# Pairwise additions of a state-space kernel's factors move to GpSimd, and its contractions take half the matmuls

## The chip, the cores and the metric

The program runs on one core of one Trainium2 chip. The metric is the device time of one execution in microseconds. TensorE (PE in the profile) multiplies, with weight loads shown as PEld; VectorE is DVE, ScalarE is ACT, GpSimd is POOL, SyncE (SP) issues most of the transfers.

## The reference

Four residual blocks on one sequence of 2048 positions and 640 channels: attention, state space (S4D), attention, state space. Both attention blocks use the same weights, and both state-space blocks the same parameters.

```python
x = x + A(layernorm(x), wqkv, wo)   # 32 heads of 20: softmax(q k^T * Dh**-0.5) v, then @ wo
x = x + B(layernorm(x), ...)        # below
x = x + A(layernorm(x), wqkv, wo)
x = x + B(layernorm(x), ...)

# B: one convolution kernel K per channel d, from 128 complex states n
A = -exp(log_A_real) + 1j * A_imag
C = (C_real + 1j * C_imag) * dt
P = exp(A * dt * arange(L))
K = 2 * einsum("dn,dnl->dl", C, P).real       # 640 x 2048
y = irfft(rfft(u, 2L) * rfft(K, 2L))[:L] + u * D_skip
```

## The kernel before

**The stages.** First comes a stretch of layer norms, transposes and the first q, k and v products; then attention one; its output product with the norm of the state-space block, and the transform of K beside it; the state-space block; and the same again without K, which is kept in DRAM (`kha`, `khb`).

**Attention.** There are 8 groups of 4 heads with 4 query blocks each, so 32 blocks; a block has 16 key tiles of 2 halves. One half is a *wave*: `scores` makes eight matmuls into a PSUM tile `S` and one exponential `pt<-S` of 128x1024 on ScalarE (L778). One attention therefore has 1024 waves. `values` (L792) multiplies the exponentials with V into `pa`. At the end of a block VectorE empties `pa` (`oc<-pa`, `oc<-oc,pa`), the row sums go through DRAM on GpSimd's DMA queue (`dn<-oc`, `dr<-dn`, then a reciprocal on VectorE, `dn<-dr`, `db<-dn`), and at the end of the next block VectorE scales (`oc<-oc,db`) and GpSimd stores (`ot<-oc`). The remaining q, k and v products run between waves as *jobs* (`m<-xh,wh` and others, L560 and L524), emptied by VectorE (`qc`, `sq`, `qhi`, `qlo`, `V`).

**The convolution kernel, `kgen`.** It runs inside attention one as a *filler*. It makes K for 32 channels at a time (20 times, index `k`), eight channels in each of 4 `sub` portions: 80 portions in all. `expand` builds a table of powers `ktab` with some thirty small VectorE operations per `k`. `left` makes, once for two portions, the complex left factors `ka` (real and imaginary part) in six VectorE operations of 128x512: four products and two operations that combine them. `right` makes four products `kb` of 128x512 by four VectorE operations, and these are not combined: `contract` lets TensorE add them up in PSUM, with four matmuls for each channel. VectorE copies the result to `ko`, and after four portions GpSimd stores it (`kd<-ko`).

```python
for c8 in range(DC // 4):
    if c8:
        yield plan.pe + 0.7, 0.43, True, ()
    plan.on_pe(0.43)
    for n in range(4):                       # ts[0..3] of right, ka re/re/im/im
        for j in range(4):
            chain(te.matmul(ps[...], a[n // 2][:, ch, :], b[n][:, dd, :], start=(n == 0), stop=(n == 3), ...))
```

**What sets the order.** A planner (`Plan`) keeps the assumed time of TensorE, ScalarE and VectorE in `pe`, `act` and `dve`, and the program is written in that order; the order is then held by dependencies without waits (`tie`, `chain`). Each VectorE operation is put down with 0.07 us plus its elements per partition over 960. `weave` takes the next step of the filler while `plan.dve < plan.pe + 0.2`. A finished portion is queued in `pend` with the time at which it is ready, and `slot` puts its contraction between two waves when that time has come and the jobs are far enough ahead (`ahead`); at most one portion waits while the next is made. `Ordered` wraps VectorE, GpSimd and SyncE: every VectorE operation is counted and ordered, on GpSimd and SyncE only transfers, memsets and `partition_all_reduce` are ordered. For each of the five blocks of q and k, `longest` calls that reduction on GpSimd (`k2m<-k`), `shift` uses its result on VectorE.

When the filler and the jobs are done, `end_jobs` frees their memory and loads the output weights (`wot`); GpSimd splits them (`woh<-wot`, `wol<-wot,woh`, L938 and L939).

Of the kernel before, what the change touches and what calls it, by code (L numbers as in the profile page):

```python
# [11 lines left out]
F32 = mybir.dt.float32  # L12
# [4 lines left out]
ALU = mybir.AluOpType  # L17
# [29 lines left out]
class Plan:  # L47


    def __init__(self):  # L50
        self.pe = self.act = self.dve = 0.0
        self.keep = False

    def on_pe(self, cost, after=0.0):
# [4 lines left out]
class Ordered:  # L59
# [4 lines left out]

    def __getattr__(self, name):
        f = getattr(self.engine, name)
        if name not in ("dma_start", "memset", "partition_all_reduce") and not self.count:
            return f

        def call(out, *a, **k):  # L70
            if self.count:
                big = a[0].shape if "reduce" in name else out.shape
                self.plan.dve = max(self.plan.dve, self.plan.pe - 0.9) + 0.07 + math.prod(big[1:]) / 960
            made = f(out, *a, **k)  # L74
            if self.plan.keep:
                self.last = self.tie(made, self.last)
            return made
        return call
# [3 lines left out]
def mha_s4d_kernel(ctx, tc, x_in, wqkv, wo, lar, aim, cr, ci, ldt, dsk,  # L82
                   c_e1, c_eb, c_f2, c_fa, c_sel, c_lv, c_id, c_sg, c_e16, c_f16, c_id16, out, parts="asas", general=None):
    nc = tc.nc
    plan = Plan()

    def tie(made, before):

        if before is not None:
            tc.add_manual_dep(made.ins, before.name, mybir.DependencyInfo(  # L90
                mybir.DependencyClass.NoSync, mybir.DependencyReason.DATA), reason="order")
        return made.ins

    se, te = nc.scalar, nc.tensor
    ve, ge, sy = (Ordered(e, plan, tie, e is nc.vector) for e in (nc.vector, nc.gpsimd, nc.sync))
# [10 lines left out]
    def pst(pool, *a, **k):  # L106
        return ps_[pool].tile(*a, **k)
# [68 lines left out]
    def chain(ins):  # L176
        last[0] = tie(ins, last[0])

    def kgen():
        NL = len(LV)  # L180
        BC, DC = 32, 8
# [59 lines left out]
        def load_powers(k):  # L241
            ge.dma_start(kpw[k % 2].rearrange("p r n d -> p (r n) d"),
                         wd[:, :, :, k * BC:k * BC + BC].rearrange("p r n d -> p (r n) d"))
# [21 lines left out]
        def views(tab, dd, hi, lo, shp):  # L265
            return ([tab[:, r, dd, hi].unsqueeze(3).to_broadcast(shp) for r in range(2)],
                    [tab[:, r, dd, lo].unsqueeze(2).to_broadcast(shp) for r in range(2)])

        def left(tab, half, out):

            shp = [P, AC, 4, 8]
            fa, fb = views(tab, slice(half * AC, half * AC + AC), slice(24, 28), slice(16, 24), shp)
            re, im = (p2.tile(shp, F32, name=f"ka{j}") for j in range(2))
            t = p3.tile(shp, F32, name="kat")
            out.extend(a.rearrange("p d h l -> p d (h l)") for a in (re, im))
            ve.tensor_mul(re, fa[0], fb[0])
            yield
            ve.tensor_mul(t, fa[1], fb[1])
            yield
            ve.tensor_sub(re, re, t)  # L280
            yield
            ve.tensor_mul(im, fa[0], fb[1])
            yield
            ve.tensor_mul(t, fa[1], fb[0])
            yield
            ve.scalar_tensor_tensor(im, im, -1.0, t, ALU.mult, ALU.subtract)
            yield

        def right(tab, neg, sub, out):

            shp = [P, DC, 8, 8]
            fa, fb = views(tab, slice(sub * DC, sub * DC + DC), slice(8, 16), slice(0, 8), shp)
            ts = [p2.tile(shp, F32, name=f"kb{j}") for j in range(4)]
            out.extend(a.rearrange("p d h l -> p d (h l)") for a in ts)
            ve.tensor_mul(ts[0], fa[0], fb[0])
            yield
            ve.tensor_mul(ts[1], neg[:, sub * DC:sub * DC + DC].unsqueeze(3).to_broadcast(shp), fb[1])
            yield
            ve.tensor_mul(ts[2], fa[0], fb[1])
            yield  # L300
            ve.tensor_mul(ts[3], fa[1], fb[0])
            yield

        def contract(r, bs, sub, ko, a, b):

            ps = pst("M", [P, 512], F32, tag=f"m{r}", name=f"m{r}")[:, :DC // 4 * NB].rearrange("p (c b) -> p c b", b=NB)
            for c8 in range(DC // 4):
                if c8:
                    yield plan.pe + 0.7, 0.43, True, ()
                plan.on_pe(0.43)  # L310
                for n in range(4):
                    for j in range(4):
                        ch, dd = DC * (sub % 2) + 4 * c8 + j, 4 * c8 + j
                        chain(te.matmul(ps[32 * j:32 * j + 32, c8, :], a[n // 2][:, ch, :], b[n][:, dd, :],  # L314
                                        start=(n == 0), stop=(n == 3), tile_position=(0, 32 * j)))
            evac = lambda: ve.tensor_copy(ko[:, 2 * sub:2 * sub + 2, :], ps)
            emptied(*((None, evac) if r else (evac,)))
            if sub == BC // DC - 1:
                ge.dma_start(kd[bs, :].rearrange("(c j) (a b) -> (j a) c b", j=4, b=NB), ko)

        NE, NSUB, AC = D // BC, BC // DC, 2 * DC
        for n in range(0, NL, 2):
# [11 lines left out]
        p3 = kw3.__enter__()  # L334
        kw2 = tc.tile_pool(name="kw2", bufs=2, side="right")
        p2 = kw2.__enter__()
        neg = p3.tile([P, BC, 8], F32, name="kneg")
# [6 lines left out]
        for k in range(NE):  # L344
            ko = p2.tile([P, BC // 4, NB], F32, name="ko")
            bs = slice(k * BC, k * BC + BC)
            for sub in range(NSUB):
                if sub % 2 == 0:
                    a = []
                    yield from left(tab, sub // 2, a)  # L350
                b = []
                yield from right(tab, neg, sub, b)
                pend.append((plan.dve, contract, (bs, sub, ko, a, b)))
                while len(pend) > 1:
                    yield "wait"
            if k + 1 < NE:
                yield from expand(k + 1, kpw[(k + 1) % 2], tab, neg)
                if k + 3 < NE:
                    load_powers(k + 3)
# [7 lines left out]
    pend = []  # L367
    free = [0.0, 0.0]
    part = [None, None]
    busy = lambda: part[0] is not None  # L370

    def emptied(*copies):

        for r, f in enumerate(copies):
            if f:
                plan.dve = max(plan.dve, plan.pe + 0.25)
                f()
                free[r] = plan.dve + 0.15
# [12 lines left out]
    def attention(x, stats):  # L391
# [218 lines left out]
        def ahead(wave):  # L610

            for (w0, c0), (w1, c1) in zip(AHEAD, AHEAD[1:]):
                if wave <= w1:
                    return c0 + (c1 - c0) * (wave - w0) / (w1 - w0)
            return c1
# [7 lines left out]
        def slot(until=None):  # L623

            if head[0] is None:
                head[0] = next(todo[0], None)
            begun = head[0] and head[0][2]
            if pend and part[0] is None and not begun and (head[0] is None or spent[0] >= ahead(len(ends) - 2)):
                t, f, args = pend[0]
                r = free.index(min(free))  # L630
                t = max(t + 0.15, free[r])
                if t <= plan.pe or until is None and head[0] is None:
                    part[:] = f(r, *args), (t, 0.43, True, ())
                    pend.pop(0)
            step = part[1] if part[0] else head[0]
            if step is None:
                return False
            t = max([step[0], *(free[r] for r in step[3])])
            if until and (t > plan.pe or plan.pe + step[1] > until):
                return False  # L640
            plan.on_pe(0.0, t)
            if part[0]:
                part[1] = next(part[0], None)
                if part[1] is None:
                    part[0] = None
            else:
                spent[0] += step[1]
                head[0] = next(todo[0], None)
            return True
# [6 lines left out]
        def need(*what):  # L656

            while not have.issuperset(what):
                if not slot():
                    assert fins  # L660
                for b in what:
                    if head[0] is None or not head[0][2]:
                        finish(b)

        with ExitStack() as c2:
# [37 lines left out]
            if first_layer:  # L703
                filler[:2] = kgen(), False
                weave(1)
            sy.dma_start(self_, c_sel)
            for i4 in range(4):
# [10 lines left out]
                for i in range(4):  # L718
                    t = xr[i] if x is None else xp.tile([P, D], F32, tag=f"xr{i}", name=f"xn{i}")
# [700 lines left out]
```

## Time and profile before

| | |
|---|---|
| three runs | 2769.9, 2770.72, 2777.75 us (median 2770.72) |
| profiled execution, span | 2775.8 us, 117573 instructions; its own time is not listed apart from its span, which lies 5.1 us above the median |
| busy: PE, ACT, DVE, POOL | 92%, 85%, 53%, 30% of the span |
| mean granted TensorE clock | 0.987 |
| attention one, first to last wave | 112 to 1146 us |
| filler: first to last contraction | 145 to 1030 us |
| output product, transform of K, state space one | 1146 to 1483 us |
| attention two, first to last wave | 1564 to 2545 us |

The shares over the whole span average stages with different limits; the stretch that matters here is from about 235 to 1030 us, in which the filler runs beside attention. A DVE, POOL or PE line of the groups with L74 stands for the helper that records every ordered operation, so groups are told apart by their tiles. A matmul of f32 operands counts as two records.

### The profile page before, as it was taken

The numbers are of one execution on the slowest core, as the hardware profiler recorded it, in microseconds if no ns is written. First come the engines' busy times: TensorE is split into PE (matmuls) and PEld (weight loads), VectorE is DVE, ScalarE is ACT, GpSimd is POOL, SyncE is SP. The second block draws the span as 40 slices with busy tenths as digits, with TensorE's granted clock in tenths as the row PEclk, the third lists the DMA queues.
The fourth block names the chain that finished last, engine by engine and source line by source line (L and its number), as shares of the span: only waits on it lengthen the run. The fifth ranks groups of instructions, "written<-read, shape, count | busy, mean of one in ns | idle before, by whom it ended". The sixth has DMA issues, their size and how long they took to land.

```text
span 2775.8 us, 117573 instructions
## 1 busy us (share of the span) xinstructions
PE 2544.2 (92%) x51968; PEld 1436.6 (52%) x51968; DVE 1469.0 (53%) x3292; ACT 2352.1 (85%) x2781; POOL 821.2 (30%) x1232
## 2 busy tenths in 40 slices
PE   7898989999999997899999998999999888878998
PEld 3453544444444442587796544544444333335988
DVE  8645778978887870366777333332222100002865
ACT  8797989999999998645665698999999999997464
POOL 1112222323223324300573022222322422222376
PEclk9999999999999999999999999999999999999999
DMA  6512232323222223354543112111211211112365
GB/s 230 162 43 68 54 77 52 85 59 78 56 68 55 57 84 96 100 202 179 198 150 92 34 49 66 54 52 51 55 50 38 69 27 38 39 40 71 106 194 159
DMA packets 179128, 238.65 MB, mean 86 GB/s; under 512 B 36144, under 2 KB 124208, under 8 KB 176816
## 3 DMA queue, kind: packets, MB, share of 16 engines
q1 hardware_dynamic: 143168, 184.44, 20.6%
q0 software_dynamic: 35440, 46.58, 7.8%
q8 instruction: 410, 6.72, 1.0%
q14 instruction: 110, 0.90, 0.1%
HBM read 154.87 MB, written 76.03 MB: 83 GB/s over the span
## 4 chain that ended last, share of the span: by engine, by line
ACT 46%; PE 28%; issue 11%; DVE 7%; DMA 6%; POOL 1%; SPq 0%; ACTq 0%; DVEq 0%; POOLq 0%
ACT pt L778 46%; PE pa L792 4%; PE S L775 3%; PE psv L1148 3%; PE po L1054 3%; PE psy L1158 2%; PE psx L1136 2%; PE psx L1113 2%; PE po L1048 1%; DMA kop<-ks 1%; PE m L314 1%; PE pv L524 1%; PE pst L1123 1%; PE m L560 1%; PE pq L681 1%
## 5 line engine op out<-in xcount | busy, mean ns | idle before, releaser
L778 ACT ACTIVATE pt<-S 128x1024 f32<-128x1024 f32 x2048 | 1930.9, 1041 | 71.8 <-PE S L775 57.2
L792 PE MATMUL pa<-pt,V 64*32 64x512 f32 x16384 | 1099.6, 594 | 0.6 <-DVE oc L74 0.6
L775 PE MATMUL S<-qop,kop 61*32 61x512 f16 x16384 | 869.4, 383 | 160.6 <-ACT pt L778 138.0
L775 PEld LDWEIGHTS <-kop 61*32 61x32 f16 x16384 | 369.9, 90 | 830.7 <-issue 726.1
L74 POOL DMA_DIRECT2D dn<-oc x256 | 125.2, 496 | 835.6 <-DVE oc L74 768.2
L792 PEld LDWEIGHTS pa<-pt,V 64*32 64x32 f32 x16384 | 308.9, 107 | 69.4 <-issue 8.3
L74 DVE COPY oc<-pa 128x512 f32<-128x512 f32 x64 | 44.2, 691 | 414.8 <-PE pa L792 414.7
L74 DVE TENSOR_SCALAR qc<-m 128x512 f32<-128x512 f32 x64 | 44.1, 689 | 289.2 <-PE m L560 289.2
L74 POOL DMA_DIRECT2D db<-dn x256 | 129.3, 511 | 139.7 <-DMA dn<-dr 137.0
L74 DVE TENSOR_TENSOR kb<-ktab 128x512 f32<-128x512 f32 x240 | 155.3, 684 | 1.5 <-PE m L314 1.5
L560 PE MATMUL m<-xh,wh 64*32 64x512 f16 x2560 | 139.1, 380 | 3.0 <-DVE qc L74 3.0
L560 PE MATMUL m<-xh,wl 64*32 64x512 f16 x2560 | 138.3, 378 | 0.7 <-issue 0.7
L560 PE MATMUL m<-xl,wh 64*32 64x512 f16 x2560 | 138.4, 378 | 0.0
L74 POOL DMA_DIRECT2D ot<-oc x256 | 130.7, 517 | 8.9 <-DVE oc L74 6.0
L314 PEld LDWEIGHTS m<-kb,ka 128*32 128x32 f32 x5120 | 79.8, 110 | 101.6 <-issue 64.5
L560 PEld LDWEIGHTS <-wh 64*32 64x32 f16 x5120 | 87.7, 94 | 75.4 <-issue 37.6
L1141 POOL TENSOR_TENSOR t<-t,kb 128x512 f32<-128x512 f32 x80 | 102.1, 1276 | 70.3 <-DVE t L74 69.4
L1125 ACT COPY xt<-pst 128x1024 f16<-128x1024 f16 x80 | 81.6, 1023 | 46.7 <-PE pst L1123 46.5
L314 PE MATMUL m<-kb,ka 128*32 128x64 f32 x5120 | 105.8, 224 | 11.4 <-DVE qc L74 11.4
L74 POOL DMA_DIRECT2D dn<-dr x64 | 35.7, 557 | 234.1 <-DVE dr L74 229.8
L1142 POOL TENSOR_TENSOR t<-t,t 128x512 f32<-128x512 f32 x78 | 99.3, 1273 | 7.3 <-DVE t L74 1.3
L970 POOL TENSOR_TENSOR ul<-u,uh 128x640 f16<-128x640 f32 x30 | 46.5, 1566 | 177.7 <-ACT uh L969 177.7
(273 smaller groups left out, 3770.4 us busy)
## 6 DMA issues: line engine op xcount, KB each, us to landing
ka<-kha SPq DMA_DIRECT2D x80, 256.0 KB
kb<-khb SPq DMA_DIRECT2D x80, 256.0 KB
db<-dn POOLq DMA_DIRECT2D x256, 64.0 KB, 2.8
kpw<-wd POOLq DMA_DIRECT2D x20, 576.0 KB, 7.7
qop<-qs SPq DMA_DIRECT2D x256, 40.0 KB
kop<-ks SPq DMA_DIRECT2D x128, 80.0 KB
ot<-oc POOLq DMA_DIRECT2D x256, 40.0 KB, 2.6
otl<-ot SPq DMA_DIRECT2D x32, 320.0 KB
```

The source lines that it names most:

```text
L74: made = f(out, *a, **k)
L314: chain(te.matmul(ps[32 * j:32 * j + 32, c8, :], a[n // 2][:, ch, :], b[n][:, dd, :], start=(n == 0), stop=(n == 3), tile_position=(0, 32 ...
L560: chain(te.matmul(ps[r][32 * t:32 * t + 32, :], a_[rows, ct, 32 * t:32 * t + 32], m[rows, ct, sl], start=(k == 0), stop=(k == 14), tile_po ...
L775: chain(te.matmul(S[32 * t:32 * t + 32, 512 * r:512 * r + 512], kt_[rows, kc + 32 * t:kc + 32 * t + 32], qt[rows, :], start=True, stop=Tru ...
L778: se.activation(pt, S, AF.Exp, scale=SCALE)
L792: chain(te.matmul(pa[r][32 * j:32 * j + 32, :], V[rows, kt, VP * h:VP * h + 32], pts[j // 2][rows, 512 * (j % 2):512 * (j % 2) + 512], sta ...
L1054: te.matmul(pos[hf], oh[:, ct, :], m[:, ct, 320 * hf:320 * hf + 320], start=False, stop=(ct == NCT - 1 and m is wol))
L1113: te.matmul(ps[:, r, i, :], e1[:, e, s, r, :], m[:, s, bs], start=(n == 0), stop=(n == 2))
L1125: se.copy(xt, pt.rearrange("p k g c -> p k (g c)"))
L1141: ge.tensor_mul(t2, t2, kb)
L1142: (ge if g0 else ve).tensor_add(t1, t1, t2)
L1148: te.matmul(pv[:, g].rearrange("p r i c -> p (r i c)"), t1[:, g * P:g * P + P], fa, start=True, stop=True)
```

## The change

`left` and `right` no longer leave all additions to VectorE and TensorE: GpSimd adds or subtracts the products in pairs. Two of the six VectorE operations of `left` go to GpSimd. `right` keeps its four VectorE products and gets two GpSimd operations, after which two combined tiles remain, and `contract` has two matmuls for each channel instead of four, put down as one portion of 0.5 us where there were two of 0.43 us. The tiles `ts[1]`, `ts[3]` and the second operands of `left` have one buffer each. The planner has a time for GpSimd (`pool`), and a portion is ready by that time. GpSimd's `tensor_add` and `tensor_sub` are ordered too, wherever they occur while the order is kept. Every VectorE operation is put down with 0.15 us instead of 0.07 us, in both attentions.

```diff
-                self.plan.dve = max(self.plan.dve, self.plan.pe - 0.9) + 0.07 + math.prod(big[1:]) / 960
+                self.plan.dve = max(self.plan.dve, self.plan.pe - 0.9) + 0.15 + math.prod(big[1:]) / 960
+            elif pool:
+                self.plan.pool = max(self.plan.pool, self.plan.dve + 0.15) + 1.3
...
         def left(tab, half, out):
-            t = p3.tile(shp, F32, name="kat")
+            t, t_ = (p3.tile(shp, F32, name=f"kat{j}") for j in range(2))
             ve.tensor_mul(re, fa[0], fb[0])
             yield
             ve.tensor_mul(t, fa[1], fb[1])
-            yield
-            ve.tensor_sub(re, re, t)
+            ge.tensor_sub(re, re, t)
             yield
             ve.tensor_mul(im, fa[0], fb[1])
             yield
-            ve.tensor_mul(t, fa[1], fb[0])
-            yield
-            ve.scalar_tensor_tensor(im, im, -1.0, t, ALU.mult, ALU.subtract)
+            ve.tensor_mul(t_, fa[1], fb[0])
+            ge.tensor_add(im, im, t_)
...
         def right(tab, neg, sub, out):
-            ts = [p2.tile(shp, F32, name=f"kb{j}") for j in range(4)]
-            out.extend(a.rearrange("p d h l -> p d (h l)") for a in ts)
+            fn = neg[:, sub * DC:sub * DC + DC].unsqueeze(3).to_broadcast(shp)
+            ts = [(p3 if j % 2 else p2).tile(shp, F32, name=f"kb{j}") for j in range(4)]
+            out.extend(a.rearrange("p d h l -> p d (h l)") for a in ts[::2])
             ve.tensor_mul(ts[0], fa[0], fb[0])
             yield
-            ve.tensor_mul(ts[1], neg[...], fb[1])
+            ve.tensor_mul(ts[1], fn, fb[1])
+            ge.tensor_add(ts[0], ts[0], ts[1])
             yield
             ve.tensor_mul(ts[2], fa[0], fb[1])
             yield
-            ve.tensor_mul(ts[3], fa[1], fb[0])
+            ve.tensor_mul(ts[3], fn, fb[0])
+            ge.tensor_sub(ts[2], ts[3], ts[2])
...
         def contract(r, bs, sub, ko, a, b):
+            plan.on_pe(0.5)
             for c8 in range(DC // 4):
-                if c8:
-                    yield plan.pe + 0.7, 0.43, True, ()
-                plan.on_pe(0.43)
-                for n in range(4):
+                for n in range(2):
...
-                pend.append((plan.dve, contract, (bs, sub, ko, a, b)))
+                pend.append((plan.pool, contract, (bs, sub, ko, a, b)))
...
-                    part[:] = f(r, *args), (t, 0.43, True, ())
+                    part[:] = f(r, *args), (t, 0.5, True, ())
```

More of the change, by code (lines that the diff above doesn't have):

```diff
@@ L50, in __init__ @@
     def __init__(self):
-        self.pe = self.act = self.dve = 0.0
+        self.pe = self.act = self.dve = self.pool = 0.0
         self.keep = False
@@ L66, in __getattr__ @@
         f = getattr(self.engine, name)
-        if name not in ("dma_start", "memset", "partition_all_reduce") and not self.count:
+        pool = name in ("tensor_add", "tensor_sub")
+        if name not in ("dma_start", "memset", "partition_all_reduce") and not self.count and not pool:
             return f
@@ L292, in right @@
             fa, fb = views(tab, slice(sub * DC, sub * DC + DC), slice(8, 16), slice(0, 8), shp)
-            ts = [p2.tile(shp, F32, name=f"kb{j}") for j in range(4)]
-            out.extend(a.rearrange("p d h l -> p d (h l)") for a in ts)
+            fn = neg[:, sub * DC:sub * DC + DC].unsqueeze(3).to_broadcast(shp)
+            ts = [(p3 if j % 2 else p2).tile(shp, F32, name=f"kb{j}") for j in range(4)]
+            out.extend(a.rearrange("p d h l -> p d (h l)") for a in ts[::2])
             ve.tensor_mul(ts[0], fa[0], fb[0])
             yield
-            ve.tensor_mul(ts[1], neg[:, sub * DC:sub * DC + DC].unsqueeze(3).to_broadcast(shp), fb[1])
+            ve.tensor_mul(ts[1], fn, fb[1])
+            ge.tensor_add(ts[0], ts[0], ts[1])
             yield
@@ L306, in contract @@
             ps = pst("M", [P, 512], F32, tag=f"m{r}", name=f"m{r}")[:, :DC // 4 * NB].rearrange("p (c b) -> p c b", b=NB)
+            plan.on_pe(0.5)
             for c8 in range(DC // 4):
-                if c8:
-                    yield plan.pe + 0.7, 0.43, True, ()
-                plan.on_pe(0.43)
-                for n in range(4):
+                for n in range(2):
                     for j in range(4):
                         ch, dd = DC * (sub % 2) + 4 * c8 + j, 4 * c8 + j
-                        chain(te.matmul(ps[32 * j:32 * j + 32, c8, :], a[n // 2][:, ch, :], b[n][:, dd, :],
-                                        start=(n == 0), stop=(n == 3), tile_position=(0, 32 * j)))
+                        chain(te.matmul(ps[32 * j:32 * j + 32, c8, :], a[n][:, ch, :], b[n][:, dd, :],
+                                        start=(n == 0), stop=(n == 1), tile_position=(0, 32 * j)))
             evac = lambda: ve.tensor_copy(ko[:, 2 * sub:2 * sub + 2, :], ps)
@@ L319, in contract @@
                 ge.dma_start(kd[bs, :].rearrange("(c j) (a b) -> (j a) c b", j=4, b=NB), ko)
+            yield from ()
         NE, NSUB, AC = D // BC, BC // DC, 2 * DC
```

## The prediction

> **What bounds the kernel now.** I read the page first, for the chain that ended last, then the windows of attention one and two, then the waits of the stretch with the filler, and last the groups by form for prices.
>
> ```profile
> span 2775.8 us, 117573 instructions
> ACT 46%; PE 28%; issue 11%; DVE 7%; DMA 6%; POOL 1%; SPq 0%; ACTq 0%; DVEq 0%; POOLq 0%
> ...
> 235.00:1030.00 795.00, 753.25 (x20788) 358.93 (x20781) 653.56 (x1427) 755.64 (x791) 235.81 (x401) 0.99 0.27 64
> 1030.00:1146.00 116.00, 88.45 (x1860) 35.99 (x1852) 8.96 (x19) 106.73 (x117) 35.91 (x58) 0.96 0.27 88
> 1685.00:2180.00 495.00, 473.97 (x11440) 229.77 (x11439) 146.57 (x278) 480.63 (x510) 121.08 (x239) 0.99 0.18 52
> ...
> 2180.00:2479.00 299.00, 172.62 (x2600) 49.29 (x2592) 298.91 (x325) 1.00 0.15 40
> ```
>
> The second block of rows is from the windows: stretch, its length, then busy time and count of PE, PEld, DVE, ACT, POOL, then clock, DMA share, GB/s. The last row is a window of the exponentials and what touches them alone. ScalarE's exponentials lead the chain with 46%. Undisturbed they take 299 / 325 = 0.920 us each. With jobs but no filler (1685 to 2180) it is 495 / 510 = 0.97; with jobs and filler (235 to 1030) 795 / 791 = 1.005. So the filler's stretch holds 795 - 791 x 0.92 = 67 us over the bare exponentials, and in it no engine has much room: PE 95% busy, ACT 95%, DVE 82%. This is all that can be won or lost there: an engine that grows past ScalarE's pace becomes the bound.
>
> ```profile
> ACT pt L778 <- PE S L775: 29.4, 21, 5.9
> ...
> DVE oc L74 <- PE pa L792: 38.2, 20, 6.9
> DVE ko L74 <- PE m L314: 30.3, 52, 1.8
> DVE qc L74 <- PE m L560: 29.0, 8, 6.9
> DVE dr L74 <- DMA dr<-dn: 14.2, 6, 4.6
> ```
>
> These are the waits of the same stretch (total, times, longest). VectorE's idle 141 us (795 - 654) are mostly waits in its fixed order for TensorE's results, 97.5 us in three rows. They can't simply be filled: an operation behind such a wait comes after it.
>
> **The change, part by part.** *Removed from VectorE.* Two of six operations of `left`, forty times each:
>
> ```profile
> L74 DVE TENSOR_TENSOR ka<-ka,kat 128x512 f32<-128x512 f32 x40 | 27.6, 690 | 1.2
> L74 DVE SCALAR_TENSOR_TENSOR ka<-ka,kat 128x512 f32<-128x512 f32 x40 | 27.4, 685 | 1.0
> L74 DVE TENSOR_TENSOR kb<-ktab 128x512 f32<-128x512 f32 x240 | 155.3, 684 | 1.5 <-PE m L314 1.5
> L314 PE MATMUL m<-kb,ka 128*32 128x64 f32 x5120 | 105.8, 224 | 11.4 <-DVE qc L74 11.4
> L1141 POOL TENSOR_TENSOR t<-t,kb 128x512 f32<-128x512 f32 x80 | 102.1, 1276 | 70.3 <-DVE t L74 69.4
> L74 DVE TENSOR_TENSOR oc<-oc,db 128x512 f32<-128x512 f32 x64 | 44.5, 695 | 24.7 <-DMA dn<-oc 22.0 <-DMA db<-dn 2.7
> ```
>
> That is 27.6 + 27.4 = 55 us, of which some 54 lie in the stretch. *Removed from TensorE:* 2560 of 5120 records, 53 us of 105.8 us busy. TensorE is late only where it, and not VectorE, sets the pace. At best the filler's stretch falls to about 0.955 per wave, between the 0.97 and the 0.92 above.
>
> *Where the work goes.* The built order of the changed kernel puts the last contraction behind 992 waves, where it stands behind 909 of 1024 now. The filler's stretch, from wave 120 (235 us), becomes 872 waves long: 872 x 0.92 = 802 us bare, 833 us at 0.955, 876 us at the present 1.005. VectorE's own work in it is 653.6 - 54 + 5 = 605 us, the 5 for two and a half more blocks of three operations of 0.7 us (`oc`).
>
> *Added to GpSimd:* 80 additions for `left` and 160 for `right`, 240 x 1.276 = 306 us, some 298 in the stretch. GpSimd was 236 of 795 us busy, so it has the time. What matters is what they do to VectorE while they run:
>
> ```profile
> 1349.32 1.28 POOL L1141 TENSOR_TENSOR t<-t,kb 128x512 f32<-128x512 f32 x1 [11.91 <-DVE t L74]
> 1350.64 0.69 DVE L74 TENSOR_TENSOR t<-t,t 128x512 f32<-128x512 f32 x1 [0.28 <-POOL t L1141]
> 1352.07 1.27 POOL L1141 TENSOR_TENSOR t<-t,kb 128x512 f32<-128x512 f32 x1 [1.46 <-DVE t L74]
> 1352.47 0.68 DVE L74 TENSOR_TENSOR x<-psx,x 128x512 f16<-128x512 f32 x1
> 2633.52 2.50 POOL L1141 TENSOR_TENSOR t<-t,kb 128x512 f32<-128x512 f32 x2 [12.02 <-DVE t L74]
> 2634.84 1.74 DVE L74 TENSOR_TENSOR t<-t,t 128x512 f32<-128x512 f32 x1 [0.22 <-POOL t L1141]
> ...
> L970 POOL TENSOR_TENSOR ul<-u,uh x30: 1394/1416/2087, 1166.2 to 2620.1; 128x640 f16<-128x640 f32 x30
> L74 DVE TENSOR_TENSOR ol<-otl,oh x32: 807/825/1674, 1126.5 to 2611.0; 128x640 fp32r<-128x640 f32 x32
> ```
>
> The first six rows are from the timeline (start, duration), the last two give the shortest, median and longest in ns. At 1350.64 VectorE's addition of two tiles in SBUF runs just after GpSimd's, and takes 0.69 us. At 2634.84 the same addition starts while GpSimd's second multiplication runs, and takes 1.74: it ends 0.56 us after GpSimd does, so it has waited. An operation with one input in PSUM (`x<-psx,x`, 1352.47) runs in the middle of a GpSimd operation and takes its usual 0.68. The last two rows show it from both sides, `ul` up to 2087 instead of 1416, `ol` up to 1674 instead of 825. So a GpSimd addition and a VectorE operation with two SBUF inputs take turns, and the price to VectorE is 1.74 - 0.69 = 1.05 us where it meets one from the start.
>
> [...]
>
> Nearly all of `kgen` is of this kind. Of the 240 additions, in VectorE's built order, 200 have such an operation directly behind the product that releases them (it has started, so GpSimd waits), and 157 have one again as the second behind (it meets the running addition). With 97.5% of them in the stretch: none blocked 605 us of VectorE work; all 234 blocked 605 + 246 = 851; the 157 in full and the other 83 for half, 605 + 161 + 42 = 808. I take 808, because the order and not the mean decides who meets whom. VectorE is 82% busy now; with later results it waits less, so I take 91%: 808 / 0.91 = 888 us, against 876 at the present pace. The ends are 833 (VectorE not the bound) and 851 / 0.91 = 935.
>
> *A cost that the diff does not show.* GpSimd loads another library where it goes from the cross-partition reduction to additions:
>
> ```profile
> 1032.16 0.72 POOL L938 CAST woh<-wot 128x640 fp32r<-128x640 f32 x1 [5.58 <-DMA wot<-in_wo]
> 1043.21 1.55 POOL L939 TENSOR_TENSOR wol<-wot,woh 128x640 fp32r<-128x640 f32 x1 [10.33 <-issue]
> 2194.41 1.53 POOL L939 TENSOR_TENSOR wol<-wot,woh 128x640 fp32r<-128x640 f32 x1 [8.95 <-issue]
> ```
>
> The built order has a library instruction ahead of `wol`, whose inputs had been ready for 10.33 us and 8.95 us. Now there is one such return in each attention. In the changed order the reductions of blocks 1 to 4 stand among the additions, so there are four more: 4 x 9.6 = 38 us of GpSimd. Queued behind each are additions, `dn`, `ot` and `kd` transfers. VectorE waits for it as soon as it writes a one-buffer tile (`ts[1]`) whose addition is outstanding, and TensorE at the contraction. After block 2 the next such product stands some ten operations behind the reduction, so nearly all is felt; after 1, 3 and 4 a whole `expand` of small operations lies between and hides half or more. I take 20 us, between 0 and 38.
>
> [...]
>
> *The sums' way through DRAM* (`dn`, `dr`, `db`, four steps on GpSimd for each block) now stands between additions that wait for products. The planner has no term for these issues. VectorE waited 14.2 us for `dr` in 6 cases; I take 6 us more, between 0 and 28 blocks x 1.3 us = 36.
>
> *The last 32 waves and the rest.* After the filler come 32 x 0.92 = 29 us. The output weights are loaded and split only there, with 11 us of GpSimd work but no library load, and the end of attention one now holds them. I take 8 us, between 0 and 16. Attention two has no filler; the higher count reorders its jobs a little: 0, within 8 either way.
>
> *Sum,* from wave 120 to the end of attention one: now 1146 - 235 = 911 us; then 888 + 20 + 6 + 29 + 8 = 951. That is +40 us: the profiled execution would go from a span of 2775.8 to 2816. The median of the runs lies 5.1 below that span, so I give 2770.7 + 40 = 2811 us.
>
> **The rivals.** *Faster.* VectorE's waits for TensorE (97.5 us) and its operations on PSUM cover the additions, and TensorE, freed of 53 us, sets a better pace. For it: the 29.4 us in which ScalarE waits for S and TensorE's 95%. Against it: the order (147 additions have two such operations in a row behind their product). It decides once fewer than about 40% of the additions block (605 + 98 = 703 us, the VectorE share of now). Time: 833 + 0 to 8 for reloads + 29 + 8 = 878, so -33; with a third of TensorE's relief lost on VectorE about -25: 2746 us.
>
> *Much slower.* Nearly all additions block, and reloads, sums and transfers queue on GpSimd so that it is the last engine at the contractions: 235.8 + 298 + 38 us of its own, and 200 x 0.6 us of waiting for started products, 692 of some 900 us in a fixed order. Then 935 + 38 + 20 + 29 + 10 = 1032, +121; at the middle between that and the forecast +85: 2856 us.
>
> *No change.* The waits saved on TensorE equal those bought: between -8 and +8, about 2771 us.
>
> **How the numbers follow.** Forecast 0.50, much slower 0.21, faster 0.22, no change 0.07. About 0.3% (8 us) is what a measurement here tells from no change. The range reaches from 2745, the faster rival's middle, to 2868, past the middle of the much slower one; about 0.1 stays out at each side. Cases of both signs don't hold equal weight: the forecast's own range is 2783 to 2845. Slower by over 0.3%: 0.71; within: 0.07; faster: 0.22.
>
> **What would show it.** In the profile after: products `kb` and `kat` with a mean well above the 684 ns of now, GpSimd additions with a mean above 1.28, together the turns; VectorE over 90% busy in the stretch; S waiting on ScalarE less and ScalarE on S more than 29.4 us; contractions that wait for GpSimd; gaps of about 9 us ahead of the addition behind each reduction, with VectorE idle behind block 2. The forecast is wrong in kind if `kb` stays near 0.7 us, or if waves in the stretch take under 0.97 us.

## The result and the profile after

The changed kernel takes 2855.66 us (median of four, 2848.19 to 2857.98) against 2771.68 us: a ratio of 1.0295, 95% interval 1.0276 to 1.0315. That is 84 us slower, where 40 were forecast. The profiled execution spans 2855.4 us, 80 more than the one before, and its own time is 2857.21.

Nearly all of it lies in attention one, which starts 3 us later and ends 80 us later than before. Page and windows of the changed kernel (stretch, length, then busy time and count of PE, PEld, DVE, ACT, POOL, clock, DMA share, GB/s):

```profile
span 2855.4 us, 112837 instructions
ACT 37%; PE 28%; DVE 18%; issue 8%; DMA 5%; POOL 3%; SPq 1%; DVEq 0%; ACTq 0%; POOLq 0%
...
239.00:1183.00 944.00, 800.66 (x19568) 361.61 (x19562) 802.27 (x1363) 823.72 (x872) 595.80 (x668) 0.96 0.23 58
1183.00:1226.00 43.00, 27.56 (x514) 9.96 (x500) 9.69 (x7) 31.03 (x34) 15.53 (x20) 0.84 0.38 133
1642.00:2624.00 982.00, 885.19 (x20720) 411.40 (x20721) 217.73 (x413) 957.33 (x1027) 239.01 (x461) 0.99 0.16 47
```

VectorE's share of the chain that ended last went from 7% to 18%. The filler's stretch, wave 120 to wave 992, takes 944 us: 1.083 per wave where it was 1.005. With the last 32 waves the attention ends 987 us after wave 120, against 911 before. Attention two takes 982 us, as before. VectorE's busy time in the stretch is 802 us, 85% of it; 808 were forecast.

The groups, by form (count, busy time, mean ns, idle time before and its releaser), show where VectorE's time went. First three lines of the kernel before, then four of the changed kernel, both over 239 to 1183 us:

```profile
L74 DVE TENSOR_TENSOR kb<-kneg,ktab 128x512 f32<-128x512 f32 x76 | 51.8, 682 | 0.0
L74 DVE TENSOR_TENSOR kat<-ktab 128x512 f32<-128x512 f32 x76 | 51.9, 683 | 0.0
L74 DVE COPY ktab<-kpw 128x192 f32<-128x192 f32 x38 | 12.9, 340 | 1.3
...
L77 DVE TENSOR_TENSOR kb<-kneg,ktab 128x512 f32<-128x512 f32 x154 | 221.4, 1437 | 28.8 <-POOL kb L77 28.8
L77 DVE TENSOR_TENSOR kb<-ktab 128x512 f32<-128x512 f32 x154 | 116.0, 753 | 0.0
L77 DVE TENSOR_TENSOR kat<-ktab 128x512 f32<-128x512 f32 x76 | 81.6, 1074 | 0.0
L77 DVE COPY ktab<-kpw 128x192 f32<-128x192 f32 x38 | 21.7, 571 | 1.3
```

`kb<-kneg,ktab` is, in the changed kernel, the second and the fourth product, the ones after which GpSimd is released. Its mean is 1437 ns where a product took 682 to 684: it is the operation that meets the running addition. Its shape is the same as before. The last line shows what the prediction did not name: a copy with only one input in SBUF lengthens too, from 340 to 571 ns. The timeline of one portion (start, duration) shows a single turn:

```profile
841.87 0.68 DVE L77 TENSOR_TENSOR kb<-ktab 128x512 f32<-128x512 f32 x1
842.47 1.75 DVE L77 TENSOR_TENSOR kb<-kneg,ktab 128x512 f32<-128x512 f32 x1
...
842.09 1.58 POOL L77 TENSOR_TENSOR kb<-kb,kb 128x512 f32<-128x512 f32 x1 [0.70 <-DVE kb L77]
```

GpSimd's addition starts at 842.09, while the third product runs, and takes 1.58 us instead of 1.28. The fourth product starts at 842.47, is done at 844.22, 0.55 us after GpSimd's end at 843.67, and takes 1.75 us. Both lose, in turn.

The library load behind the reduction of block 4, from the timelines of GpSimd, VectorE and ScalarE:

```profile
800.56 0.37 POOL L77 PARTITION_ALL_REDUCE k2m<-k  x1 [7.92 <-issue]
...
812.69 1.87 POOL L77 DMA_DIRECT2D kpw<-wd  x1 [0.96 <-issue]
822.95 1.25 POOL L77 TENSOR_TENSOR ka<-ka,kat 128x512 f32<-128x512 f32 x1 [8.38 <-issue]
...
814.28 0.68 DVE L77 TENSOR_TENSOR kb<-ktab 128x512 f32<-128x512 f32 x1
826.19 2.48 DVE L77 TENSOR_SCALAR dr<-dr 128x16 f32<-128x16 f32 x1 [11.22 <-DMA dr<-dn]
...
830.24 1.02 ACT L781 ACTIVATE pt<-S 128x1024 f32<-128x1024 f32 x1 [10.96 <-PE S L778]
```

GpSimd stands 8.38 us ahead of an addition. Behind that addition waits its transfer `dr<-dn` (issued at 824.16), so VectorE, whose order has `dr` next, waits 11.22 us for it, and ScalarE gets no scores for 10.96 us. Here the wait went through a transfer and not through a one-buffer product. The first row shows a second gap: GpSimd stands 7.92 us ahead of the reduction as well, for nothing that the profile shows. Three reductions of the stretch have such a gap, 21.2 us together. The prediction counted the way back from a reduction only; that these gaps are loads too is likely, but not shown.

ScalarE's and TensorE's waits in the stretch (total, times, longest):

```profile
ACT pt L781 <- PE S L778: 114.2, 70, 11.0
...
PE S L778 <- ACT pt L781: 50.1, 137, 1.2
PE m L316 <- POOL kb L77: 43.8, 31, 9.4
PE m L316 <- DVE qc L77: 28.6, 12, 9.0
```

ScalarE waited 29.4 us for scores before, now 114.2. TensorE stands in front of contractions, for GpSimd and for PSUM that VectorE has not emptied. The granted clock fell with it, to 0.96 in the stretch and 0.84 behind it, from 0.99 and 0.96. Two of the prediction's signs did not come: VectorE is 85% busy and not over 90%, and TensorE's scores wait more for ScalarE (18.6 us before), not less.

### The profile page after: what moved, and what is told of

Read it like the earlier page. It is cut to its first block, busy times and chain, and to the rows that moved or that the text cites. A ratio compares the mean times of both kernels' runs of the same rounds, so it can differ in the third digit from the quotient of the medians.

```text
span 2855.4 us, 112837 instructions
## 1 busy us (share of the span) xinstructions
PE 2533.6 (89%) x49408; PEld 1414.2 (50%) x49408; DVE 1625.9 (57%) x3212; ACT 2344.4 (82%) x2781; POOL 1174.3 (41%) x1472
## 4 chain that ended last, share of the span: by engine, by line
ACT 37%; PE 28%; DVE 18%; issue 8%; DMA 5%; POOL 3%; SPq 1%; DVEq 0%; ACTq 0%; POOLq 0%
ACT pt L781 35%; DVE kb L77 7%; PE pa L795 5%; PE S L778 3%; PE psv L1151 3%; PE po L1057 2%; PE psy L1161 2%; PE psx L1139 2%; PE psx L1116 2%; DVE kat L77 2%; PE pv L527 1%; POOL kb L77 1%; PE pq L684 1%; PE po L1051 1%; PE pst L1126 1%
## 5 line engine op out<-in xcount | busy, mean ns | idle before, releaser
L795 PE MATMUL pa<-pt,V 64*32 64x512 f32 x16384 | 1115.4, 600 | 4.0 <-DVE oc L77 2.4
L778 PEld LDWEIGHTS <-kop 61*32 61x32 f16 x16384 | 379.0, 90 | 904.8 <-issue 804.6
L795 PEld LDWEIGHTS pa<-pt,V 64*32 64x32 f32 x16384 | 311.5, 107 | 81.0 <-issue 16.6
L77 POOL TENSOR_TENSOR kb<-kb,kb 128x512 f32<-128x512 f32 x160 | 232.4, 1457 | 98.7 <-DVE kb L77 64.0
L77 DVE TENSOR_TENSOR kb<-kneg,ktab 128x512 f32<-128x512 f32 x160 | 232.0, 1450 | 28.8 <-POOL kb L77 28.8
L77 POOL TENSOR_TENSOR ka<-ka,kat 128x512 f32<-128x512 f32 x80 | 123.2, 1544 | 74.5 <-DVE kat L77 47.5
L316 PE MATMUL m<-kb,ka 128*32 128x64 f32 x2560 | 63.0, 235 | 75.6 <-POOL kb L77 43.8
L77 DVE TENSOR_TENSOR kb<-ktab 128x512 f32<-128x512 f32 x160 | 121.2, 757 | 0.0
```

The source lines that it names most:

```text
L316: chain(te.matmul(ps[32 * j:32 * j + 32, c8, :], a[n][:, ch, :], b[n][:, dd, :], start=(n == 0), stop=(n == 1), tile_position=(0, 32 * j)))
L778: chain(te.matmul(S[32 * t:32 * t + 32, 512 * r:512 * r + 512], kt_[rows, kc + 32 * t:kc + 32 * t + 32], qt[rows, :], start=True, stop=Tru ...
L795: chain(te.matmul(pa[r][32 * j:32 * j + 32, :], V[rows, kt, VP * h:VP * h + 32], pts[j // 2][rows, 512 * (j % 2):512 * (j % 2) + 512], sta ...
```

## The experiments

Ratios are to the kernel before, from runs on the same chip.

**No library loads.** In attention one the reductions of blocks 1 to 4 are left out; GpSimd copies each partition's own maximum instead:

```diff
-            ge.partition_all_reduce(k2m, k2, P, bass.bass_isa.ReduceOp.max)
+            if local:
+                made = ge.engine.tensor_copy(k2m, k2)
...
+            else:
+                ge.partition_all_reduce(k2m, k2, P, bass.bass_isa.ReduceOp.max)
```

> The changed kernel, but in attention one the cross-partition maximum of blocks 1 to 4 is left out: GpSimd copies each partition's own maximum instead, so that no library has to be loaded between the additions. Theory (turns on the port for most of the loss, the library loads for some 30 us of it): 2822 to 2832 us, no gaps of 7 to 9 us behind the reductions, pace of waves 256 to 288 and 640 to 672 back from 1.50 and 1.42 to about 1.03. Rival (turns and a late last contraction alone; the loads lie beside other work): 2848 to 2858. Second rival (the loads are the larger half): under 2810.

Measured: 2835.53 us, ratio 1.0208 (1.0191 to 1.0225). The reductions with their loads are worth 0.87% or 24 us, a little under the theory's 30. The time lies 3.5 us above the theory's range and 12 or more from both rivals. The pace of the two groups of waves came back to 1.16 and 1.15 us only, not to 1.03. Row of the stretch:

```profile
238.00:1159.00 921.00, 794.45 (x19596) 361.41 (x19592) 810.04 (x1363) 824.20 (x873) 593.48 (x669) 0.98 0.25 60
```

Without loads the stretch takes 921 us, 23 less, and VectorE is busy for 810 us of it, 88%.

**Small additions.** Each addition covers 2 elements of a partition, and the rest of the sums is left out, for example:

```diff
-            ge.tensor_add(ts[0], ts[0], ts[1])
+            ge.tensor_add(*(ts[n][:, :1, :1, :2] for n in (0, 0, 1)))
```

> The changed kernel, but each of the 240 additions covers 2 of 512 elements of each partition; the rest of the additions is left out. Library loads, waits and order stay. Theory (turns): VectorE's products come back to about 0.68 us, 2790 to 2805 us, what is left being loads and the late end. Rival (the planner's new order carries the loss): 2840 to 2858. Rival (loads carry it): within 10 us of the changed kernel.

Measured: 2772.48 us, ratio 0.9977 (0.9965 to 0.9989): faster than the theory's 2790 to 2805, and far from both rivals. With small additions everything that the change costs, and a little more, is gone, though the planner's order and the loads are still there.

**Both at once.**

> Both cuts of the two kernels before at once: additions of 2 elements, and no cross-partition maximum in blocks 1 to 4 of attention one. What is left of the change is its order and TensorE's halved contractions. Theory: 2755 to 2775 us, about the kernel before, since the relief of TensorE is partly lost to the later end of the filler. Rival (halved contractions pay where GpSimd costs nothing): 2735 to 2750. Rival (the order itself costs): 2790 or more.

Measured: 2759.15 us, ratio 0.9927 (0.9911 to 0.9944), within the theory's range, though by the ratio it is 20 us faster than the kernel before and not "about" it. What remains of the change here is the halved contractions, the two operations of `left` that VectorE no longer makes (54 us of its busy time), and the new order. Together they are worth 0.7% where GpSimd has next to nothing to do; this run does not part them. Its row of the stretch:

```profile
235.00:1085.00 850.00, 776.98 (x19616) 358.38 (x19616) 611.98 (x1360) 820.04 (x873) 350.08 (x669) 0.99 0.27 65
```

VectorE's 612 us are what the prediction had for "none blocked", 605.

**The count alone** (0.15 instead of 0.07 in the kernel before).

> The kernel before with one edit: 0.15 us instead of 0.07 us for each VectorE operation in the plan. Theory (the count is a minor part): within 15 us of the kernel before, 2765 to 2786 us, with a filler that ends later. Rival (the count, by stretching the filler to the end of attention one, carries a third of the loss or more): 2800 us or more.

Measured: 2807.9 us, ratio 1.0102 (1.0085 to 1.0119), the rival's side. Two windows, before and behind wave 960:

```profile
244.00:1059.00 815.00, 769.49 (x20700) 363.74 (x20693) 590.44 (x1287) 788.30 (x833) 240.64 (x413) 0.99 0.26 62
1059.00:1142.00 83.00, 45.08 (x1225) 24.00 (x1232) 70.66 (x138) 31.11 (x35) 24.44 (x27) 0.71 0.24 79
```

The first 833 waves go at 0.978, better than the 1.005 of the kernel before. Then eight contractions that the planner could not place before wave 992 come in a lump, and 35 waves take 83 us. The changed kernel does not pay this: its last contraction just fits, and its last 32 waves take 43 us. The run shows that the count trades pace against the end of the filler.

**Does TensorE's wait for the sum cost anything?** The additions go into a tile that nobody reads, and the contractions take the first and third product without the sums:

```diff
-            ge.tensor_add(ts[0], ts[0], ts[1])
+            ge.tensor_add(scr, *(ts[n].rearrange("p d h l -> p (d h l)") for n in (0, 1)))
```

> The changed kernel, but GpSimd's 240 full additions write into a tile that nobody reads; the contractions take the first and third products as VectorE leaves them, so half of the products is left out of the result and no contraction waits for GpSimd. The turns on the port stay, and so does VectorE's wait before it overwrites a product that GpSimd still reads. Theory (what the turns cost is VectorE's time, whoever waits for the sum): 2838 to 2856 us. Rival (the loss beyond VectorE's own time is TensorE standing in front of a contraction whose addition is late): 2800 to 2830 us.

Measured: 2846.89 us, ratio 1.025 (1.0233 to 1.0267), so 0.45% or 12 us less than the changed kernel. The theory holds: of TensorE's 43.8 us in front of additions most is not gained when the wait goes, because TensorE then stands elsewhere for VectorE.

**GpSimd busy, but only writing.** Memsets of the second operand, then an addition of 2 elements; the rest of the sums is left out:

```diff
-            ge.tensor_add(ts[0], ts[0], ts[1])
+            ge.memset(ts[1], 0.0); ge.memset(ts[1], 1.0)
+            ge.tensor_add(*(ts[n][:, :1, :1, :2] for n in (0, 0, 1)))
```

> The changed kernel, but each addition is replaced by two GpSimd memsets of the second operand, 512 elements each, and an addition of 2 elements behind them: GpSimd is busy for about as long, the contraction waits as long, but in nearly all of that time GpSimd only writes. The rest of the additions is left out. Theory (reading ports in turns): products near 0.68 us, 2772 to 2790 us, as with the additions of 2 elements or slightly above. Rival (any GpSimd work of that length costs, by lateness or by a port of any kind): 2815 us or more.

Measured: 2811.81 us, ratio 1.012 (1.0103 to 1.0137), between the two and close to the rival. VectorE's products came back to 683 and 681 ns, so the turns come with GpSimd's reading (the runs show the turns alone, not the port on which the expectations put them), and 1.75% (48 us) go with it. But 1.4% (40 us) more than with small additions remained, which the theory had not. VectorE waited 60.6 us for GpSimd in this kernel. Buffers were the first guess.

**Three buffers** in turn for the second and fourth product together, instead of one each, in the write-only kernel and in the full change:

```diff
-            ts = [(p3 if j % 2 else p2).tile(shp, F32, name=f"kb{j}") for j in range(4)]
+            ts = [p3.tile(shp, F32, tag="kbt", bufs=3, name=f"kb{j}") if j % 2 else p2.tile(shp, F32, name=f"kb{j}") for j in range(4)]
```

> The kernel with memsets in place of the additions (most of the additions left out), now with three buffers in turn for the second and fourth product instead of one each. With one each it took 2812 us against 2772 with additions of 2 elements, though its products took 0.68 us. Theory (those 40 us are VectorE waiting before it overwrites a product that GpSimd still holds): 2778 to 2795 us, and VectorE's wait for GpSimd of 61 us in the stretch falls under 20. Rival (they are contractions and transfers that come late behind GpSimd's queue): 2803 to 2815.

> The changed kernel in full, with three buffers in turn for the second and fourth product instead of one each. Theory (the turns on the port bound VectorE whatever it waits for): 2840 to 2856 us. Rival (the one-buffer waits are a term of their own beside the turns): 2810 to 2832.

Measured: 2817.61 us (1.0152, 1.0136 to 1.0169) and 2854.78 us (1.0282, 1.0265 to 1.03). Neither gained anything that counts: the guess was wrong for the write-only kernel, and in the full change the third buffer is no term. VectorE's waits from 238 to 1097 us in the write-only kernel, with one buffer each and with three in turn, say why:

```profile
DVE ko L77 <- PE m L316: 55.4, 44, 3.2
DVE kb L77 <- POOL kb L77: 51.6, 24, 8.2
...
DVE ko L77 <- PE m L316: 80.1, 45, 7.0
DVE kb L77 <- POOL kb L77: 25.8, 8, 7.8
```

The wait for GpSimd halved, and VectorE stood as much longer in front of the contractions' results, some of which wait for GpSimd in their turn. The wait only moved.

**Write-only without loads**, with the memsets and without the reductions of blocks 1 to 4.

> The kernel with memsets in place of the additions (most of the additions left out) and, besides, no cross-partition maximum in blocks 1 to 4 of attention one, so no library loads between. With loads it took 2812 us, 40 more than with additions of 2 elements, and more buffers changed nothing. Theory (a busy GpSimd makes each library load longer for those who wait, and that is the larger part of the 40): 2770 to 2785 us. Rival (a busy GpSimd hands over portions and sums late all along): 2795 to 2812.

Measured: 2782.81 us, ratio 1.002 (1.0009 to 1.0031). The time is in the theory's range, but not for the theory's reason. The loads are worth 1.0% (28 us) in the write-only kernel, against 0.5% (14 us) with small additions, so a busy GpSimd makes them 14 us dearer, the smaller part of the 40. The remaining 0.93% (26 us) over the kernel with small additions and no loads is GpSimd's time as such. Products at 684 ns again, VectorE busy for 621 us:

```profile
235.00:1106.00 871.00, 781.20 (x19532) 358.53 (x19532) 620.86 (x1367) 818.92 (x870) 558.08 (x1123) 0.98 0.26 63
```

**The count back** (0.07 in the changed kernel; last contraction behind wave 859).

> The changed kernel with 0.07 us instead of 0.15 us in the plan; the last contraction then stands behind 859 waves instead of 992. Theory (the turns bound the filler, so that a denser plan gets the same work done in about the same time, and the later 130 waves run free): 2835 to 2860 us. Rival (the larger count, and with it the late end, is part of the loss): 2805 to 2830. Rival (denser work meets more turns): over 2865.

Measured: 2942.93 us, ratio 1.0596 (1.0577 to 1.0615): the last rival's side, far above its bound. Row of its stretch:

```profile
240.00:1164.00 924.00, 738.48 (x17618) 337.78 (x17600) 791.12 (x1339) 716.13 (x753) 578.40 (x623) 0.93 0.24 60
```

The rival's reason, more turns, hardly shows: the second and fourth products take 1500 ns, against 1437, and VectorE's work is 791 us in all. The theory's first half held, since the filler takes about as long as in the changed kernel (924 us, VectorE 86% busy, against 944). But only 753 waves pass in it, and the waves behind the filler still have to run, which the theory did not add up. This points to the bound: with turns the filler needs some 920 to 945 us, and the larger count only lets more waves pass beside it. No count between the two was run with the additions on GpSimd.

**The additions on VectorE**, with three counts. In `left` and `right` `ge` becomes `ve`, and a portion is ready at `plan.dve`.

> The changed kernel with the 240 additions on VectorE: no turns, no library loads between them, and a portion is ready by VectorE's time in the plan. VectorE gets 240 x 0.60 = 144 us in a stream instead of some 200 us of blocked time. Theory: 30 to 60 us faster than the changed kernel, 2795 to 2825, since the planner now counts these operations and the filler can end too late. Rival (the planner's count makes the filler miss the end of attention one): 2840 us or more.

> The additions on VectorE, contractions halved, and 0.05 us for each VectorE operation in the plan, so that the last contraction stands behind 919 waves. With 0.15 us eleven or so contractions stood behind wave 992 and cost some 105 us there, while wave 960 came 33 us sooner than in the kernel before. Theory (halved contractions pay once GpSimd has no part in it and the filler ends in time): 2740 to 2762 us. Rival (the denser plan books VectorE beyond its time, and TensorE waits for it): 2775 us or more.

> The additions on VectorE, contractions halved, 0.08 us for each VectorE operation in the plan; one contraction stands behind wave 992, the one before it behind 989. At 0.05 us it took 2791 us, with a pace of 1.0 us per wave in the middle, at 0.15 us 2854 with 0.95 and a late filler. Theory (between the two the filler just ends and the pace is better than at 0.05): 2765 to 2785 us, no better than the kernel before beyond a few us, because VectorE has 144 us more to do. Rival (halved contractions pay here): under 2760.

Measured: 2854.28 us at 0.15 (1.0271, 1.0253 to 1.0288), 2790.85 at 0.05 (1.0059, 1.0042 to 1.0076), and 2766.49 at 0.08 (0.9959, 0.9945 to 0.9973). The first two came out on the rivals' side, the third in the theory's range. At 0.15 the first 832 waves from wave 120 go at 0.963, and then the rest of the filler comes in a lump:

```profile
242.00:1043.00 801.00, 732.51 (x18354) 343.72 (x18345) 638.16 (x1326) 780.46 (x832) 236.73 (x410) 0.99 0.26 61
1043.00:1180.00 137.00, 42.26 (x1032) 21.60 (x1031) 122.95 (x247) 30.18 (x33) 18.94 (x24) 0.63 0.16 42
```

At 0.08 it just ends, and this version is the fastest of the complete kernels, 0.4% (11 us) under the kernel before:

```profile
236.00:1105.00 869.00, 787.01 (x19824) 366.13 (x19817) 765.65 (x1598) 831.13 (x883) 265.82 (x445) 0.99 0.26 64
```

VectorE has 766 us of work in it, 44 less than the changed kernel without loads (810), and no addition to wait for: here an addition on VectorE costs VectorE less than the same addition on GpSimd.

**The count alone, smaller** (0.10 in the kernel before).

> The kernel before with 0.10 us instead of 0.07 us for each VectorE operation in the plan; in its built order the last contraction stands behind 959 waves, where 0.15 us put eight of them behind wave 992. Theory (the larger count spaces VectorE's work better, and the loss at 0.15 us was the filler that did not end): 2750 to 2765 us, faster than the kernel before. Rival (the count as such costs): 2780 us or more.

Measured: 2784.48 us, ratio 1.002 (1.0009 to 1.0031). The theory missed, there is no gain from spacing; the number lies on the rival's side, but by the ratio the loss is 0.2%. So the gain at 0.08 above does not come from the count alone. It is put down to the halved contractions, with their single portion in the plan; no run shows these by themselves.

## Why the prediction was right in kind and wrong in size

**Sums.** The ratios lead from the kernel before to the change in four steps, each in per cent and, of 2772 us, in microseconds: halved contractions, fewer VectorE operations and order -0.73% (-20); GpSimd's time, only writing, +0.93% (+26); its reading, +1.88% (+52); the library loads, +0.87% (+24). The sum is +2.95%, 82 us. The steps depend on their order: loads are 0.5% with small additions and 1.0% in the write-only kernel.

**VectorE's work: right in the sum.** 605 us were forecast without turns, 612 measured; 808 with turns, 802 to 810 measured. The single turn shown costs 1.07 us where 1.05 was taken. The 157 turns of 240 additions were not measured as such: in the trace of the changed kernel 145 of the 480 products take over 1.2 us. Part of the sum comes from operations that the count left out, such as the copies at 571 instead of 340 ns, so the close fit has some luck in it.

**The step that failed: 808 / 0.91 = 888 us.** I let VectorE's later results shorten its waits and took it 91% busy. Without loads the stretch took 921 us at 88%, and with the dense plan 86%. 33 of the 36 us that are missing on the way from 951 to 987 lie here. In those 921 us VectorE stands idle for 111 us, where 91% of 888 left 80. Its three waits for TensorE did shorten, from 97.5 to 57 us, as I had argued. But 16.6 us of waiting for GpSimd's additions came in, and only part of the old waits went.

What I overlooked is that GpSimd's time costs something as such. I gave it room because it was 236 of 795 us busy, and priced only its turns, the loads and 6 us for the sums. The write-only kernel without loads shows that this time alone costs 26 us, though the products are not slowed: ScalarE's wait for scores goes from 25.8 us, in the kernel with small additions and no loads, to 47.9, and VectorE's for GpSimd from 4.9 to 46.2. It fits the missing 33, but that the same 26 us stand in the full change, where VectorE has 190 us more to do, is argued and not shown. One more buffer in turn is not the way out: in the write-only kernel with loads it halved VectorE's wait for GpSimd and gained nothing (2818 against 2812). That transfers behind the additions hand over late, as `dr` does above, was seen in single places, not measured by itself. So the size of the failed step is known, and its cause is open in part.

**Library loads: right in size, by another route.** 20 us were taken, 23 measured in the stretch. That nearly all is felt behind block 2 was right (waves 256 to 288 fell from 1.50 to 1.16 us without loads); that an `expand` hides half or more of block 4's was not: it cost 0.27 us in each of the 32 waves from 640, some 9 us, through `dr`. The gaps behind the reductions were 7 to 8.4 us, less than the 9 to 10 of before, and gaps of 6 to 8 us ahead of three reductions were not in the sum at all. The 6 us for the sums' way through DRAM were not measured: VectorE's wait for `dr` is 14.3 us now and was 14.2, and 11.2 of it is the one load above.

**TensorE's relief: smaller than its best case.** I gave 833 us as the end without VectorE as the bound. The kernel with small additions and no loads, which is that case, takes 850. TensorE's time in the contractions fell from 105.8 to 63.0 us, 43 less and not 53. Over those 850 us the full additions cost 921 - 850 = 71 us, of which 21 are GpSimd's time (871 - 850) and 50 its reading (921 - 871); the sum had 888 - 833 = 55 for both.

**The end: nearly right.** 43 us for the last 32 waves, 37 forecast. **Attention two: right**, unchanged.

**Rivals.** The faster one needed VectorE's work near 703 us; it was 802 to 810, so it is out, and so is "no change". The much slower one, at 2856 us, names the measured time almost exactly, but by luck. Its +85 is said to be the middle between +121 and +40, which is 80.5 or 2851 us. And its condition, nearly all additions blocking with 851 us of VectorE work, did not come; only turns, loads and GpSimd's queue together did.

## What to carry to other kernels

Work moved from VectorE to GpSimd was not taken from VectorE here: 230 additions in the stretch cost VectorE 198 us (810 against 612) on GpSimd and 154 us (766 against 612) on VectorE itself. Where both engines read SBUF, price such a move by the VectorE operation that meets it, found in the built order (1437 ns on the mean instead of 682 here), and add what a busy GpSimd delays in its queue (26 us in the write-only kernel without loads) and each library change that new neighbours force (here gaps of 7 to 8.4 us behind a reduction, and of 6 to 8 us ahead of three of them, whose cause was not shown). When the sum of work on an engine is known, be careful with its utilization in a fixed order: VectorE went from 82% to 85 to 88% here, not to 91%. And where a planner's count fixes an order, test the change with the count tuned again: here the same halved contractions go from 3% slower to 0.4% faster by the engine that adds and the count.

## What the runs showed of the hardware that was not expected

VectorE's copies with a single SBUF source are held up too: `ktab<-kpw` of 128x192 went from 340 to 571 ns on the mean, and one `dr<-dr` of 16 elements, the guard ahead of a reciprocal, took 2.48 us beside two GpSimd additions, where the one at 410.02 us of the same trace took 0.17. In the write-only kernel GpSimd memsets of 512 elements (about 530 ns) held up no product, 683 and 681 ns beside them, but the same copies a little: 390 ns.

In these stretches the granted TensorE clock was the lower, the less TensorE was busy; what lowers it was not shown. It was 0.99 in the stretch of the kernel before (TensorE 95% busy), 0.96 with the change (85%), 0.63 in the lump of the filler at the end of attention one with the additions on VectorE (31%).
